# Another written order for the first 28 steps of a windowed-attention and feed-forward kernel

## The chip, the cores and the metric

The kernel runs on one core of a Trainium2 chip. The metric is the device time of one launch in microseconds (us); three runs of the kernel before the change took 841.5, 842.04 and 842.22 us. The core has five engines with their own instruction queues: PE (matrix products and the loads of their weights, which the profile lists as PEld), DVE (vector operations), ACT (activations and scaled copies), POOL, and SP, which in this kernel only issues transfers between the off-chip memory and the core. Each engine takes its instructions strictly in the order of its own queue and waits at an instruction until the semaphores that it names have been raised.

## The reference

Attention over 8 batches of 8 heads (576 positions, head width 64) with two kinds of window, and a feed-forward block with a gate on what comes out of it:

```python
scores = scale * np.matmul(q, k.transpose(0, 1, 3, 2))
mask_plain = (rel >= 0) & (rel < window)
mask_dil = (rel >= 0) & (rel < window * dilation) & (rel % dilation == 0)
...
attn = np.exp(scores - max) / sum
x = np.matmul(attn, v)            # 4608 tokens x 512
...
h = x @ w_in                      # 512 x 2048
g = h * np.clip(h + 3.0, 0.0, 6.0) / 6.0
return g @ w_out                  # 2048 x 512
```

## The kernel before

The attention is cut into 48 pieces called trios (192 positions of one kind of window for four heads each). The feed-forward block works on 12 chunks of 384 tokens, and its 2048 hidden columns are cut into 16 slices of 128. A step is one slice for one chunk: a first product (`gemm1`, 12 matrix products of 384 columns, L536 to L538), a gate on ACT and DVE (L544, L547, L551, L555), and a second product (`gemm2`, 9 products of 512 columns, L586 to L588). All large products are made from a high and a low half of each operand, three products for one.

A chunk can enter its first step only when the trios with its tokens have gone through attention and the slice of the weights has been loaded and converted. So the start of the kernel is a tangle of three chains, and its order is written out by hand: the string `ORDER` (L58 to L82), 588 names, is walked from left to right (L1275), and each name issues the instructions of one operation. ACT, DVE, SP and PE take their instructions in exactly the order in which they are issued there. What comes behind the first 28 steps is put in order by a planner (`_in_time`) and is not touched.

The names of `ORDER`, with t for a trio, m for a step and p for a half slice of the weights:

- On PE: `B`t makes the scores of trio t (L219, on top of a mask product at L328) and, from t = 2 on, between them the weighted values of an earlier trio (L229; `FOLLOW` at L57 names it). With one of the two it is 98 instructions, weight loads counted, with both 194, of 32 or 64 rows each. `V`t makes values alone (96). `E`t and `Y`t are three transposes each (L345, 6 instructions): of the exponents, and of the attention's output. `G`m is the first product of step m (24 instructions), `H`m the second (18).
- On DVE and ACT, for a trio: `R`, `S`, `X` (maximum, difference, exponent: L256, L260, L283), `CA` (copy of the transposed exponents, L358), `Z` (division by the sum, L304 to L307), `CX` (copy of the transposed output, L362), `XH`, `XL` (its high and low half, L438 and L444).
- On DVE and ACT, for half a slice of weights: `U`, `Q` (L490, L494, on ACT), `s`, `j`, `a` (L498, L504, L511, on DVE), `h` (L514, ACT) and `l` (L520, DVE). `RE`, `T`, `GH`, `GL` are the gate of a step.
- On SP: `k`t and `v`t load a trio's queries with keys and its values (416 and 390 KB; the tiles `first`, from t = 9 on `kq` and `v`), `w`p loads half a slice of weights (512 KB, tile `st`), `M0`, `M1`, `M2` three pieces of the masks (160, 24 and 432 KB). A name like `w0@R1` makes the transfer wait for `R1`. The transposes need `M1`, from which POOL makes the identity matrix (L762).

In the order before, the first four steps on PE are G0, G1, G2, G3, with B9 between G1 and G2 and B10 and B11 around G3; the first second product is H0.

Of the kernel before, what the change touches and what calls it, by code (L numbers as in the profile page):

```python
# [55 lines left out]

FOLLOW = {2: 0, 3: 1, 4: 2, 5: 3, 7: 5, 8: 6, 9: 7, 10: 8, 11: 9}  # L57
ORDER = """  # L58
k0 M0 M1 k2 k1 v0 k3 v2 B0 v1 k5 R0 S0 X0 E0 B1 CA0 B2 R1 S1 w0@R1 X1 Z0 E1 k4@X1 R2 CA1 Y0 v4@CA1 B3 S2 CX0 XH0
k6@S2 X2 XL0 v6@XL0 v3@XL0 Q0 U0 E2 s0 Z1 CA2 B4 R3 j0 S3 w2@j0 a0 X3 v5@a0 h0 Y1 Z2 B6 CX1 XH1 R4 Y2 R6 E3 CX2 XL1  # L60
CA3 S6 XH2 B5 S4 X6 w4@XH2 XL2 X4 Q2 l0 E6 U2 Z3 E4 k7@E6 CA6 R5 CA4 Y3 v7@CA6 s2 V4 CX3 S5 k8@CX3 XH3 j2 X5 XL3
v8@j2 Q4 E5 Z4 U4 w13@E5 CA5 a2 Y4 B7 s4 CX4 w6@a2 j4 h2 XH4 l2 k9@j4 B8 Z5 k10@l2 R7 Y5 XL4 w7@R7 CX5 Z6 G0 Q13 XH5
S7 w1@Q13 Q6 R8 X7 XL5 Y6 U6 S8 E7 G1 CX6 a4 CA7 s6 XH6 j6 X8 h4 XL6 B9 w5@G1 RE0 a6 RE1 l4 h6 k11@RE1 T0 E8 Q7 Z7
G2 CA8 GH0 R9 Q1 v9@GH0 GL0 U1 S9 U7 Y7 T1 B10 X9 s1 CX7 l6 GH1 v10@CX7 j1 XH7 E9 G3 R10 RE2 CA9 XL7 Q5 S10 U5 Z8
B11 X10 RE3 a1 GL1 h1 E10 T2 Y8 CA10 Z9 CX8 V10 GH2 R11 XH8 Y9 l1 CX9 Z10 H0 XH9 XL8 XL9 w3@XL8 S11 Y10 G8 GL2 CX10
w16@S11 T3 X11 s5 XH10 s7 GH3 XL10 E11 RE8 GL3 G6 CA11 j5 U3 w28@CA11 T8 Q3 a5 GH8 G10 j7 RE6 w11@GH8 h5 GL8 U16 T6
l5 Q16 G4 s16 GH6 a7 RE10 Q28 j16 v11@a7 h7 T10 H2 w8@j16 Q11 a16 U28 l7 h16 s3 H3 s28 GH10 GL6 l16 RE4 j3 Q8
w30@RE4 V11 U8 T4 GL10 GH4 G20 w17@U8 Z11 GL4 w9@Z11 a3 Y11 s8 RE20 G13 j28 CX11 h3 T20 XH11 j8 Q30 H4 XL11 U30 l3
w29@Q30 GH20 a8 Q17 a28 U17 H1 GL20 RE13 s17 h8 T13 Q9 j17 GH13 H8 U9 l8 w31@GH20 h28 GL13 Q31 a17 U31 G12 s9 l28
h17 Q29 j9 U29 l17 w14@GL20 G25 Q14 a9 RE12 s31 h9 s30 T12 U14 H20 l9 RE25 s14 GH12 T25 GL12 G5 w15@T25 j14 GH25 j31  # L70
GL25 a14 H13 RE5 a31 h14 T5 Q15 l14 U15 H12 j30 GH5 h31 s15 GL5 j15 G18 l31 w23@j14 Q23 a15 a30 h15 G11 s29 RE18 l15
h30 T18 l30 w18@U15 GH18 H10 j29 RE11 GL18 T11 a29 Q18 G27 GH11 U18 GL11 h29 s18 H18 l29 w19@T18 Q19 RE27 j18 U19
T27 a18 GH27 H25 s19 h18 GL27 l18 w10@Q18 Q10 U10 j19 H11 U11 s10 a19 s11 h19 j10 G22 l19 w12@a19 j11 a10 G15 RE22
a11 h10 T22 h11 l10 GH22 H6 l11 w20@j10 Q12 RE15 GL22 Q20 T15 U20 G14 GH15 s20 U12 GL15 j20 U13 s12 H22 RE14 a20 T14
h20 s13 GH14 l20 w21@l11 G7 Q21 GL14 U21 j13 j12 G24 a13 RE7 a12 h13 T7 h12 l13 w22@l20 H14 GH7 RE24 l12 GL7 T24 G17
s21 Q22 j21 GH24 U22 GL24 a21 U23 G16 RE17 s22 s23 h21 T17 j22 GH17 G9 l21 w24@l12 Q24 a22 U24 j23 h22 H24 s24 l22
j24 w25@l22 a23 H15 RE16 GL17 h23 a24 RE9 T16 h24 l23 G26 GH16 T9 Q25 GL16 U25 l24 w27@GH16 GH9 s25 G19 j25 a25 H17
h25 Q27 l25 H16 RE26 GL9 w26@H17 k12 k13 v12 v13 M2 RE19 T26 T19 G21 GH26 GH19 Q26 H9 U26 s26 U27 j26 H7
RE21 GL26 a26 T21 h26 GL19 H5 GH21 l26 GL21 s27 j27 G23 a27 h27 H21 l27 RE23 T23 GH23 H19 GL23 H23
"""  # L80


# [1456 lines left out]
```

## Time and profile before

| what | value |
|---|---|
| median of 3 runs | 842.04 us |
| the profiled execution | 846.16 us, of which the span of the trace is 844.0 us |
| mean granted PE clock | 0.990 |
| busy share of the span: PE, DVE, ACT, POOL | 98%, 77%, 68%, 7% |
| share of the chain that ended last that is PE's | 96% |
| PE instructions: products, weight loads | 8758, 8758 |
| read from and written to off-chip memory | 174.47 MB, 38.80 MB |

The span runs from the first to the last instruction in the trace; 2.2 us of the profiled execution lie around it. The rows of a view by stretches give for each engine its busy time and, in brackets, how many instructions fell into the stretch, then the granted PE clock, the busy share of the transfer engines and their rate.

### The profile page before, as it was taken

What the parts mean: (1) busy time and instruction counts of PE and PEld (TensorE: products, weight loads), DVE (VectorE), ACT (ScalarE), POOL (GpSimd) and SP (SyncE); (2) the same over time, 40 slices, a digit from 0 to 9 for tenths busy, and PEclk for the clock granted to TensorE, in tenths of its full rate; (3) what the DMA queues carried; (4) which work ended last, traced back from release to release, by engine and by line L of the source; (5) the groups of instructions that cost most, each with busy time, mean ns of one, the idle gap of its engine ahead of it and who ended that gap; (6) DMA issues with size and microseconds to landing.
All of it is one profiled execution on the core that took longest, in us unless ns stands there. A gap on an engine that the chain in (4) does not pass through costs nothing.

```text
span 844.0 us, 22143 instructions
## 1 busy us (share of the span) xinstructions
PE 828.2 (98%) x8758; PEld 776.8 (92%) x8758; DVE 646.7 (77%) x1313; ACT 573.7 (68%) x1400; POOL 55.5 (7%) x114
## 2 busy tenths in 40 slices
PE   7799999999999999999999999999999999999998
PEld 4589999898888889899899999999999999999997
DVE  4799988556677898888898777888677798445983
ACT  3688776334799885789985598855698755445552
POOL 0000000010222211000400001000001000000000
PEclk8799999999999999999999999999999999999999
DMA  8848332343778899899986898977789766996381
GB/s 280 275 134 251 124 122 84 115 152 115 229 233 267 290 345 378 280 391 392 389 295 233 285 347 298 340 249 258 272 313 319 255 228 234 336 368 219 131 293 57
DMA packets 115767, 214.70 MB, mean 254 GB/s; under 512 B 7504, under 2 KB 40272, under 8 KB 115664
## 3 DMA queue, kind: packets, MB, share of 16 engines
q1 hardware_dynamic: 115664, 213.29, 73.1%
q8 instruction: 69, 1.13, 0.5%
q14 instruction: 34, 0.28, 0.1%
HBM read 174.47 MB, written 38.80 MB: 253 GB/s over the span
## 4 chain that ended last, share of the span: by engine, by line
PE 96%; ACT 2%; issue 1%; DVE 1%; DMA 0%; SPq 0%; DVEq 0%
PE ps_o L736 28%; PE ps_x L745 9%; PE ps_x L747 9%; PE ps_x L746 9%; PE ps_h L536 6%; PE ps_h L537 5%; PE ps_h L538 5%; PE ps_o L586 5%; PE ps_o L588 5%; PE ps_o L587 5%; PE ps_b L237 2%; PE ps_a L219 1%; PE ps_a L229 1%; PE ps_b L219 1%; PE ps_a L237 1%; PE ps_a L345 1%
## 5 line engine op out<-in xcount | busy, mean ns | idle before, releaser
L736 PE MATMUL ps_o<-gh,ring 128*128 128x384 f32 x896 | 230.9, 334 | 0.5 <-ACT gh L1195 0.5
L736 PEld LDWEIGHTS ps_o<-gh,ring 128*128 128x128 f32 x896 | 161.9, 188 | 0.8 <-ACT gh L1195 0.8
L736 PE MATMUL ps_o<-gl,ring 128*128 128x384 f32 x448 | 149.9, 335 | 0.3 <-DVE gl L1199 0.2
L1199 DVE TENSOR_TENSOR gl<-g,gh 128x384 fp32r<-128x384 f32 x224 | 116.5, 553 | 28.2 <-ACT gh L1195 26.0
L1195 ACT CAST gh<-g 128x384 fp32r<-128x384 f32 x224 | 104.3, 513 | 27.8 <-PE ps_o L736 20.3
L745 PE MATMUL ps_x<-x,ring 128*128 128x384 f32 x256 | 88.5, 346 | 0.0
L536 PE MATMUL ps_h<-x,wi 128*128 128x384 f32 x256 | 88.3, 345 | 0.0
L537 PE MATMUL ps_h<-x,wi 128*128 128x384 f32 x256 | 86.4, 338 | 0.0
L538 PE MATMUL ps_h<-x,wi 128*128 128x384 f32 x256 | 86.4, 337 | 0.0
L746 PE MATMUL ps_x<-x,ring 128*128 128x384 f32 x256 | 86.2, 337 | 0.0
L747 PE MATMUL ps_x<-x,ring 128*128 128x384 f32 x256 | 86.1, 336 | 0.0
L736 PEld LDWEIGHTS ps_o<-gl,ring 128*128 128x128 f32 x448 | 84.1, 188 | 0.9 <-DVE gl L1199 0.9
L586 PE MATMUL ps_o<-wo,gh 128*128 128x512 f32 x192 | 75.1, 391 | 0.0
L587 PE MATMUL ps_o<-wo,gh 128*128 128x512 f32 x192 | 74.7, 389 | 0.0
L588 PE MATMUL ps_o<-wo,gl 128*128 128x512 f32 x192 | 74.7, 389 | 0.0
L544 ACT ACTIVATE t<-ps_h,three 128x384 f32<-128x384 f32 x64 | 37.0, 582 | 49.8 <-PE ps_h L538 49.0
L747 PE MATMUL ps_x<-cell,ring 128*128 128x384 f32 x192 | 64.8, 338 | 0.0
L746 PE MATMUL ps_x<-cell,ring 128*128 128x384 f32 x192 | 64.7, 337 | 0.0
L745 PE MATMUL ps_x<-cell,ring 128*128 128x384 f32 x192 | 64.7, 337 | 0.0
L1164 DVE TENSOR_TENSOR g<-g 128x768 f32<-128x768 f32 x64 | 60.8, 952 | 0.0
L547 DVE SCALAR_TENSOR_TENSOR t<-t,ps_h 128x384 f32<-128x384 f32 x64 | 35.0, 548 | 29.1 <-ACT t L544 28.7
L1049 DVE TENSOR_TENSOR s<-ps_x,s 128x384 f32<-128x384 f32 x64 | 35.2, 550 | 24.5 <-ACT s L1042 20.4
(114 smaller groups left out, 1765.4 us busy)
## 6 DMA issues: line engine op xcount, KB each, us to landing
ring<-sums SPq DMA_DIRECT2D x112, 512.0 KB, 8.0
ring<-rights SPq DMA_DIRECT2D x112, 512.0 KB, 6.7
st<-in_w SPq DMA_DIRECT2D x32, 512.0 KB, 4.1
kq<-in_qk SPq DMA_DIRECT2D x39, 416.0 KB, 4.8
v<-in_v SPq DMA_DIRECT2D x39, 390.0 KB, 5.8
sums<-wi SPq DMA_DIRECT2D x24, 256.0 KB, 7.1
rights<-wo SPq DMA_DIRECT2D x24, 256.0 KB, 5.4
out<-o SPq DMA_DIRECT2D x16, 384.0 KB, 2.9
```

The source lines that it names most:

```text
L536: nc.tensor.matmul(ph, lhsT=wt(f, 0)[:, ks], rhs=a, start=(kt == 0), stop=False)
L537: nc.tensor.matmul(ph, lhsT=wt(f, 0)[:, ks], rhs=b, start=False, stop=False)
L538: ins = nc.tensor.matmul(ph, lhsT=wt(f, 1)[:, ks], rhs=a, start=False, stop=(kt == NK - 1))
L586: nc.tensor.matmul(po[c][tt], lhsT=gh[:, rows], rhs=wt(f, 2), start=first, stop=False)
L587: nc.tensor.matmul(po[c][tt], lhsT=gh[:, rows], rhs=wt(f, 3), start=False, stop=False)
L588: return nc.tensor.matmul(po[c][tt], lhsT=gl[:, rows], rhs=wt(f, 2), start=False, stop=(f == NF - 1))
L736: nc.tensor.matmul(banks[part][:, :CH], lhsT=right[:, a, cols], rhs=x, start=(start and not i), stop=(i == 2), skip_group_check=True)
L745: nc.tensor.matmul(bank, lhsT=tile_[:, 0, ks], rhs=h[:, kt], start=(start and kt == 0), stop=False, skip_group_check=True)
L746: nc.tensor.matmul(bank, lhsT=tile_[:, 0, ks], rhs=l[:, kt], start=False, stop=False, skip_group_check=True)
L747: nc.tensor.matmul(bank, lhsT=tile_[:, 1, ks], rhs=h[:, kt], start=False, stop=(kt == 1), skip_group_check=True)
L1195: nc.scalar.copy(two[0], gated_tile(g, q, k))
L1199: nc.vector.tensor_tensor(out=two[1], in0=gated_tile(g, q, k), in1=two[0].bitcast(F32), op=ALU.subtract)
```

## The change

Only the string `ORDER` is another. It holds the same 588 names, so every instruction and every transfer is there as before; what changes is where each stands in its engine's queue, and which of the transfers wait for which operation. The first line of the old table and of the new one:

```diff
-k0 M0 M1 k2 k1 v0 k3 v2 B0 v1 k5 R0 S0 X0 E0 B1 CA0 B2 R1 S1 w0@R1 X1 Z0 E1 k4@X1 R2 CA1 Y0 v4@CA1 B3 S2 CX0 XH0
+k0 M0 k1 B0 R0 w6 k2 M1 U6 v3 S0 X0 v0@R0 B1 w2@B1 R1 E0 S1 X1 s6 E1 CA0 v1 U2 k3 B2 j6 CA1 s2 R2 w0 B3 S2 Z0 Q6 k6 Q2
...
```

On SP, the first transfers before were the following rows; here `in_qk` is a `k`, `in_v` a `v`, `in_w` a `w` and `in_mask` a piece of the masks:

```order
L190 DMA first<-in_qk 128x832
L759 DMA mi<-in_mask 32x2560
L759 DMA mi<-in_mask 96x128
L190 DMA first<-in_qk 128x832 x2
L199 DMA first<-in_v 128x780
L190 DMA first<-in_qk 128x832
L199 DMA first<-in_v 128x780 x2
L190 DMA first<-in_qk 128x832
L475 DMA st<-in_w 128x1024
```

And after the change:

```order
L190 DMA first<-in_qk 128x832
L759 DMA mi<-in_mask 32x2560
L190 DMA first<-in_qk 128x832
L475 DMA st<-in_w 128x1024
L190 DMA first<-in_qk 128x832
L759 DMA mi<-in_mask 96x128
L199 DMA first<-in_v 128x780 x2
L475 DMA st<-in_w 128x1024
L199 DMA first<-in_v 128x780
L190 DMA first<-in_qk 128x832
L475 DMA st<-in_w 128x1024
```

The first load of weights (now `w6`) moved from the eleventh transfer to the fourth, two more (`w2`, `w0`) stand among the first twelve, `M1` moved from the third to the sixth, and `k3`, which was the seventh, is now the eleventh.

On PE, the first product G0 stood before behind block B8, the last one that reads a tile `first`, and the transposes Y5 (`x` is the output of attention, `ps_h` the bank of the first product):

```order
L229 MATMUL ps_a<-first,a 32x65
L219 MATMUL ps_a<-first 32x64
L345 MATMUL ps_a<-ident,x 128x128 x3
L536 MATMUL ps_h<-x_78,wi 128x384
L537 MATMUL ps_h<-x_84,wi 128x384
L538 MATMUL ps_h<-x_78,wi 128x384
```

After the change the first product is G1, and this stands ahead of it:

```order
L229 MATMUL ps_a<-first,a 32x65
L219 MATMUL ps_a<-kq 32x64
L345 MATMUL ps_a<-ident,e 128x128 x3
L536 MATMUL ps_h<-x_78,wi 128x384
L537 MATMUL ps_h<-x_84,wi 128x384
L538 MATMUL ps_h<-x_78,wi 128x384
```

One more block, B9, which reads `kq`, and the transposes E7, Y6 and E8 have moved ahead of the first product. In PE's queue the blocks and transposes follow each other now as B0 B1 E0 E1 B2 B3 Y0 B6 E3 E2 B5 Y1 B4 Y3 E5 Y2 B7 E6 E4 V4 B8 E7 Y4 Y5 Y6 B9 E8, then G1 Y7 B10 E9 G0 Y8 B11 G2 Y9 E10 G3 V10 E11 and then G6. Before they were B0 E0 B1 B2 E1 Y0 B3 E2 B4 Y1 B6 Y2 E3 B5 E6 E4 Y3 V4 E5 Y4 B7 B8 Y5, then G0 Y6 E7 G1 B9 E8 G2 Y7 B10 E9 G3 B11 E10 Y8 V10 Y9 and then H0.

At the head of ACT's queue the first exponent stood alone; now a conversion of weights (L490, `U6`) stands ahead of it, and `U2`, `Q6`, `Q2` and `U0` stand among the operations of trios 0 to 3.

More of the change, by code (lines that the diff above doesn't have):

```diff
@@ L58 @@
 ORDER = """
-k0 M0 M1 k2 k1 v0 k3 v2 B0 v1 k5 R0 S0 X0 E0 B1 CA0 B2 R1 S1 w0@R1 X1 Z0 E1 k4@X1 R2 CA1 Y0 v4@CA1 B3 S2 CX0 XH0
[L60 to L78, printed above, removed]
@@ L79 @@
-RE21 GL26 a26 T21 h26 GL19 H5 GH21 l26 GL21 s27 j27 G23 a27 h27 H21 l27 RE23 T23 GH23 H19 GL23 H23
+k0 M0 k1 B0 R0 w6 k2 M1 U6 v3 S0 X0 v0@R0 B1 w2@B1 R1 E0 S1 X1 s6 E1 CA0 v1 U2 k3 B2 j6 CA1 s2 R2 w0 B3 S2 Z0 Q6 k6 Q2
+j2 U0 w16@U2 s0 w4 R3 Y0 CX0 k5@S0 S3 j0 Q0 B6 X3 X2 v2@X2 Z1 U4 E3 a2 k4 s4 R6 E2 CA3 j4 U16 B5 S6 Q4 v6 v5@CA0 CA2
+Y1 h2 a4 B4 Z3 Y3 R5 CX1 XH1 l2 h4 S5 X6 X5 l4 E5 Z2 XH0 R4 k7@Z3 XL1 a0 CX3 S4 CA5 XH3 Y2 CX2 B7 v4 v8@X2 E6 XL3 XH2
+X4 k8@j4 w28@XH3 CA6 R7 v7@XH0 E4 XL0 S7 XL2 CA4 V4 a6 Z5 B8 Q28 Z4 h0 Z6 R8 X7 s16 E7 w1@s4 k9@a6 Y4 U28 S8 w3 Y5 l0
@@ new lines @@
+CA7 CX4 Y6 B9 XH4 w30@Z5 XL4 R9 X8 Z7 U30 U3 CX5 S9 k10@XH4 E8 G1 Y7 k11 M2 CA8 B10 X9 XH5 s28 s30 h6 j16 CX7 s3 XL5
+l6 Z8 XH7 RE1 j3 E9 G0 Q3 Y8 Q16 v9@S8 CA9 w5@B10 CX6 j30 XL7 R10 T1 v10 S10 CX8 B11 XH6 Z9 v11@XH7 G2 Q30 R11 XL6 X10
+Y9 w8@B11 RE0 E10 T0 S11 XH8 G3 RE2 CX9 XH9 CA10 X11 Q1 V10 T2 RE3 XL8 E11 XL9 a16 j28 Q5 w14@Q30 w18 h16 G6 GH1 Q14
+G4 RE6 U1 T3 a28 Z10 G8 T6 w17@CA10 a3 l16 a30 h28 U5 GH0 CA11 l28 V11 RE4 h3 w7@E9 s1 T4 U14 j1 RE8 Z11 h30 G13 T8 U8
+RE13 Q8 a1 Y11 w10@Q8 Y10 s14 G25 CX11 GL0 h1 GH4 G10 U17 Q7 s8 T13 RE25 l3 l1 H0 U7 j14 w31@h1 s17 j8 CX10 a14 w29
@@ new lines @@
+l30 T25 G20 a8 GL1 RE10 h8 T10 h14 l8 Q17 Q18 l14 RE20 s7 s5 GL4 T20 GH3 w9 XH10 U9 H1 j7 j17 a7 GL3 h7 G5 s9 Q9 w15
+l7 U29 j5 a17 H4 a5 U18 G12 s18 RE5 GH2 j18 H3 G11 G27 h17 U31 RE12 Q29 h5 j9 U10 s29 T5 a18 T12 GH8 l5 w19@H3 GH12
+GL8 s10 h18 U15 GH20 GL2 a9 s31 XL10 RE27 U19 j31 l18 j29 RE11 h9 T27 GH25 Q19 H2 s15 j15 H8 l17 w20@U10 T11 a29 GL20
+h29 GL25 G18 Q15 l29 j10 RE18 s19 w22@Q29 j19 Q10 G22 a10 T18 a15 l9 U20 h10 h15 w11@s29 GL12 GH13 a19 H20 Q31 RE22
+G15 w12@G18 l15 H25 GH11 T22 l10 s20 U22 GL11 a31 RE15 w13 U11 h31 s22 h19 G14 s11 T15 j20 Q20 a20 l19 j11 H12
@@ new lines @@
+w21@GL11 GH6 l31 Q11 h20 G7 a11 RE14 GL6 H11 j22 w25 Q12 Q22 T14 RE7 U12 GH22 l20 T7 s12 Q21 j12 GL22 GL13 H6 a12 a22
+U13 w24@Q20 Q13 GH10 s13 GH18 h12 GL18 G17 h11 l11 G24 RE17 h22 U21 l12 H18 H13 RE24 j13 s21 G9 T17 j21 T24 GL10 Q25
+U25 l22 a13 s25 H10 h13 RE9 GH24 v12@RE9 l13 a21 h21 U24 T9 G26 G16 GL24 j25 l21 Q24 GH14 RE26 w23@h20 a25 s24 j24
+GH27 Q23 U23 a24 RE16 s23 h25 w26@l13 T26 GL14 j23 a23 H24 T16 l25 h24 GH15 H22 G19 GH16 GL16 GH9 GL9 h23 w27@Q24 U26
+l24 H14 Q26 G21 RE19 GL15 RE21 H16 l23 U27 s26 Q27 j26 a26 h26 T19 s27 l26 GH19 H9 GH17 H15 GH5 T21 G23 j27 GH21 GL21
@@ L80 @@
+GL19 a27 GL5 XH11 RE23 T23 GH7 H19 GL7 h27 GH23 H21 GH26 k13@H9 v13@G21 XL11 GL17 l27 GL27 H5 H7 k12@GH19 GL23 GL26
+H23 H17
 """
```

## The prediction

> **What bounds the kernel now.** I read the page first, then the view of waits, for the time behind 58 us and for the first 60 us.
>
> ```profile
> PE 828.2 (98%) x8758; PEld 776.8 (92%) x8758; DVE 646.7 (77%) x1313; ACT 573.7 (68%) x1400; POOL 55.5 (7%) x114
> ```
>
> PE is the bound. Behind 58 us it waits twice, for 0.7 us in all:
>
> ```profile
> PE ps_o L736 <- ACT gh L1195: 0.5, 1, 0.5
> PE ps_o L736 <- DVE gl L1199: 0.2, 1, 0.2
> ```
>
> All that an order of the first steps can win or lose lies ahead of that. There the same view says (engine, line, what was waited for, us, times, longest):
>
> ```profile
> PE ps_a L219 <- issue: 3.8, 3, 1.5
> PE ps_a L345 <- ACT e L283: 1.9, 1, 1.9
> PE ps_a L229 <- issue: 1.4, 1, 1.4
> PE idle L162 <- DVE zeros L159: 1.3, 1, 1.3
> PE ps_a L345 <- DVE x L307: 1.3, 3, 0.7
> PE ps_a L229 <- ACT a L358: 1.3, 3, 0.7
> ```
>
> The largest item, 5.2 us, is "issue": PE waits for nothing that is in the program. The chain of work shows where:
>
> ```profile
> 18.57 1.49 issue
> ...
> 24.41 0.94 issue
> ...
> 28.93 1.39 issue
> ...
> 36.15 1.36 issue
> ```
>
> I cut the time at the ends of these four waits (20.06, 25.35, 30.31, 37.51) and let the view by stretches count instructions:
>
> ```profile
> 1.30:15.23 13.93, 11.57 (x219) 6.79 (x222) 4.16 (x9) 2.93 (x6) 0.29 (x1) 0.75 0.86 310
> 15.23:20.06 4.83, 2.68 (x136) 2.05 (x136) 2.93 (x8) 2.69 (x6) 0.00 (x0) 1.00 0.93 285
> 20.06:25.35 5.29, 3.99 (x127) 2.88 (x127) 5.09 (x13) 4.30 (x12) 0.00 (x0) 1.00 0.77 257
> 25.35:30.31 4.96, 3.31 (x127) 2.65 (x127) 4.25 (x12) 4.05 (x11) 0.00 (x0) 1.00 0.75 220
> 30.31:37.51 7.20, 5.16 (x126) 3.44 (x126) 5.44 (x15) 3.18 (x8) 0.00 (x0) 0.60 0.97 337
> 37.51:45.98 8.47, 8.46 (x126) 8.01 (x127) 5.79 (x13) 5.36 (x12) 0.00 (x0) 0.73 0.60 201
> ```
>
> From one wait to the next there are 127 products and 127 weight loads, then 127 and 127, then 126 and 126: nearly the same number each time, though the program does something else in each. The page has a queue that fits:
>
> ```profile
> q8 instruction: 69, 1.13, 0.5%
> ```
>
> 1.13 MB in 69 packets is 16.4 KB each. I conclude that PE's instructions come in blocks of about 256, and that from 15.23 to 37.51 the next block came too late four times. **The attention part is paced by the supply of instructions**: 4.83, 5.29, 4.96 and 7.20 us for a block. The first three average 5.03. The slow one is the stretch in which transfers held their engines for 0.97 of the time.
>
> [...]
>
> **The change, part by part.** No instruction is added or removed. From the order of PE I count instructions. Before, the block edges seen above are numbers 449 (in B3), 705, 961, 1217 and 1473 (in B8), and H0 begins with number 2470. After, number 449 is again in B3, 31 behind its start, and 1729 is in B9, 1985 in B10, 2241 in B11; G6 begins with 2476. Ahead of G6 stand the same operations as ahead of H0 before, plus E11 (6 instructions). So I compare the start of G6 with the start of H0 plus one E, from these rows:
>
> ```profile
> 50.23 0.33 PE ps_a L345 x3
> ...
> 57.38 0.94 PE ps_a L229 x46
> 58.32 0.48 PE ps_a L345 x3
> 58.80 0.41 PE ps_o L586
> ```
>
> 58.80 and 0.33: **59.1 us** is what the new order has to beat. Behind it PE's work is the same, and it hardly waits.
>
> *To number 449.* B3 needs `k3`, now the eleventh transfer. Up to it go four `k`, three `v`, two `w`, M0 and M1: 4 x 416 + 3 x 390 + 2 x 512 + 184 = 4,042 KB or 4.14 MB. At the 310 GB/s of the first stretch from 1.30 on they are there at 14.7, and 31 instructions later it is 15.0; before it was 15.23. This hides the other edits at the start. U6 ahead of the first exponent X0 waits for the fourth transfer, 1.54 MB, at about 6.3. M1, now sixth, is there after 1.99 MB at 7.7, and `v0`, the eighth, after 2.79 MB at 10.3. Each may hold up E0 or B2 by about a microsecond, but B3 cannot start ahead of 14.7 anyway; without that cover they would cost that microsecond. The conversions that come earlier fall where DVE and ACT are busy for 4.16 and 2.93 of 13.93 us, so I cost them at nothing.
>
> *The waits that transfers now have.* SP's queue stands still at each of them, so I ask whether the loads behind it still come in time.
>
> ```profile
> L511 DVE CUSTOM_DVE_ANT_0 va<-va 128x1024 uint16<-128x1024 uint16 x32 | 21.4, 683 | 0.1
> ...
> L256 DVE TENSOR_REDUCE mx<-ps_a 128x6 f32<-128x384 f32 x12 | 6.6, 550 | 8.5 <-PE ps_a L219 8.3
> L260 DVE TENSOR_TENSOR e<-ps_a,mx 128x384 f32<-128x384 f32 x12 | 6.5, 552 | 0.1
> L283 ACT ACTIVATE e<-e 128x384 f32<-128x384 f32 x12 | 6.2, 522 | 10.4 <-DVE e L260 10.4
> ...
> L444 DVE TENSOR_TENSOR x<-xf,x 128x96 fp32r<-128x96 f32 x12 | 3.5, 330 | 0.0
> ```
>
> ```profile
> kq<-in_qk SPq DMA_DIRECT2D x39, 416.0 KB, 4.8
> ...
> first<-in_v SPq DMA_DIRECT2D x9, 390.0 KB, 5.2
> ```
>
> The tightest is `v2@X2`, with `k4`, `v6` and `v5` behind it. X2 stands behind X3 on ACT, and X3 waits for B3, whose other 163 instructions end at 16.4 to 17.1. R3, S3, X3 and X2 (0.55, 0.55, 0.52, 0.52) make it 18.5 to 19.2, `v2` lands 5.2 later, `k4` about one more: 24.7 to 25.4. B4 waits for both, and its instruction 961 is due at 25.1 by the sum below: between nothing and 0.7 late. `k9@a6` holds B9 in the same way. B7 ends about a microsecond behind number 1217, on DVE R7, S7 and XL0 at 0.55, XL2 in three pieces at 0.33 and a6 (L511) at 0.68 take 3.4, the load 4.8: 9.2 behind 1217, where 1729 is due 10.1 behind it. I give them no term of their own; the one slow block of the sum below is where such a wait goes, and a second one is a rival.
>
> *From 449 to 2241.* Seven refills. Before, four followed each other at this pace, because G0 comes behind only 1,648 instructions; now G1 comes behind 1,860, and G1 and G0 are alone between blocks. Does the work fit under the refill? A pair block and a product of 384 columns at full clock are:
>
> ```profile
> 54.67:56.27 1.60, 1.60 (x99) 1.33 (x98) 1.60 (x4) 1.38 (x3) 0.00 (x0) 1.00 0.08 22
> ```
>
> ```profile
> 48.13 0.18 PE ps_h L536
> 48.30 0.17 PE ps_h L537
> ```
>
> From 1729 to 1985: 125 of 194 instructions of B9 (1.03), E8 (0.33), G1 (12 x 0.175 = 2.10), Y7 (0.33), 95 of B10 (0.78): 4.57 us. From 1985 to 2241 it is 4.58 in the same way. Both are under the fastest refill, 4.83, so these two are still paced by the refill and no faster than that. I take 4.83 for them, since the rate of transfers fell to 0.60 by then before. The other five lie in the time of heavy loading. The bounds for one are 4.83 and 7.20; before, one of four was slow. I take four at 5.03 and one at 7.20. The sum: 15.0 + 20.1 + 7.2 + 9.7 = 52.0.
>
> *From 2241 to G6.* 73 of 194 of B11 (0.60), G2 and G3 (4.20), Y9, E10, E11 (0.99), V10 (0.94): 6.7 us.
>
> **The sum** is 58.7, against 59.1: **0.4 us less**. What before lost at low clock and in waits behind 37.51 is won, and the three more blocks at the refill's pace give it back. The profiled execution took 846.16 us (span 844.0) and would take 845.8; on the median of 842.04 I carry over the difference: **841.6 us**. I call 0.2% (1.7 us) about what a measurement can tell.
>
> **The rivals.**
>
> *No slow block* (chance 0.29). The slow one before fell into a stretch in which PE also waited for data; if it was that, the five take 5.03 each, and the sum is 56.5, 2.6 less: 839.4. With all seven at 4.83 it would be 55.5: 838.4, the lower end. Against it: the transfers are as many and are packed no less.
>
> *Low clock at the first products* (0.15, the slower side). Before, PE ran at low clock in a stretch around G0:
>
> ```profile
> 30.00:40.00 10.00, 7.64 (x222) 5.76 (x223) 6.34 (x18) 3.49 (x9) 0.00 (x0) 0.59 0.98 346
> ```
>
> ```profile
> 32.06 0.87 PE ps_a L345 x3
> 32.93 0.43 PE ps_a L328
> ...
> 35.37 0.43 PE ps_a L328
> ...
> 41.34 0.32 PE ps_h L536
> ```
>
> Then a product takes 0.32 instead of 0.175, a pair block 2.44 (from 32.93 to 35.37), three transposes 0.87. While blocks wait for their instructions that costs nothing. But from 1729 on, at 42.3 in my sum, the work up to 1985 would be 1.57 + 0.87 + 3.84 + 0.87 + 1.19 = 8.3 us instead of 4.83: 3.5 more, 845.1 us. The point from which it decides: low clock still on behind 42.3. Before, it ended at about 42. For it speaks that the thin stretches, PE busy about half of the time, go on longer now.
>
> [...]
>
> *A second slow block* (0.10): 7.20 instead of 5.03, 2.2 more, 843.8, just slower. It decides from two of seven on.
>
> *Refills hidden* (0.03). Then the transfers would bound: twelve `k`, nine `v`, nine `w`, M0 and M1 up to `k11`, 13,294 KB or 13.6 MB, at 310 GB/s 45.2 us; with B11 (1.60) and the 6.1 us behind it that is 53: about 836. The four waits of before speak against it.
>
> **How the numbers follow.** The forecast has 0.43 and stays within 0.2%. Faster are the first and the last rival: 0.32. Slower are the low clock and the second slow block: 0.25. The range of 838.8 to 845.1 takes in each case's own time but the last, and leaves out the fastest part of the first.
>
> **What would show it.** In the profile after: waits called issue on PE, each about 254 instructions behind the one before, some six in B6, B4, B7, B8, B9 and B10; number 449 at about 15; the first L536 at 43 to 44; G6 (the fifth group of twelve products) at 58.7; no wait of PE behind it that was not there before. It would be wrong if the stretches between the waits were not of equal count, if B9 or B10 waited for a transfer for over a microsecond, or if DVE came late for a second product behind 59 us.

## The result, and the profile after

The kernel after took 850.48 us (median of 6 runs, 849.12 to 851.95), the kernel before beside it 842.13 us (6 runs, 840.75 to 843.72). The ratio is 1.0097, with a 95% interval of 1.008 to 1.0115: **1% slower**, where the forecast was 841.6 us and the range ended at 845.1.

The page of the profile after, first row:

```profile
PE 828.8 (98%) x8758; PEld 777.3 (92%) x8758; DVE 646.8 (76%) x1313; ACT 572.7 (68%) x1400; POOL 56.1 (7%) x114
```

PE is still the bound and as busy as before. The view of waits of PE, over the whole span (engine, line, what was waited for, us, times, longest):

```profile
PE ps_a L219 <- issue: 6.3, 3, 2.8
PE ps_a L345 <- POOL ident L762: 2.6, 1, 2.6
PE idle L162 <- DVE zeros L159: 1.3, 1, 1.3
PE ps_a L219 <- DMA first<-in_qk: 1.1, 2, 0.9
PE ps_a L229 <- DMA first<-in_v: 1.1, 1, 1.1
PE ps_a L229 <- ACT a L358: 0.6, 1, 0.6
PE ps_o L736 <- ACT gh L1195: 0.5, 1, 0.5
```

The waits for instructions are there (6.3 us), and a new one of 2.6 us: E0 waits for the identity matrix, which POOL makes from M1. Behind the first 63 us PE waits as little as before. I cut the time at the block edges, that is where PE goes from one block of 256 instructions into the next (numbers 449, 705, 961 and so on to 2497; in the first profile of before the four waits for instructions end at 705, 961, 1217 and 1473, each 256 behind the one before). These numbers count all instructions in PE's queue, also the 27 ahead of H0 that are neither products nor weight loads and mostly wait for a semaphore. The prediction left these out, so that H0, its number 2470, is number 2497 here. The view by stretches says:

```profile
1.30:16.20 14.90, 10.00 (x219) 5.59 (x225) 4.73 (x9) 4.80 (x9) 0.64 (x1) 0.86 0.93 325
16.20:22.70 6.50, 3.73 (x137) 2.91 (x138) 5.47 (x14) 3.27 (x7) 0.00 (x0) 0.76 0.81 295
22.70:28.65 5.95, 5.95 (x127) 4.28 (x126) 3.77 (x9) 3.14 (x7) 0.00 (x0) 0.50 0.67 250
28.65:34.04 5.39, 3.50 (x132) 2.59 (x128) 5.30 (x13) 5.19 (x15) 0.00 (x0) 0.96 0.88 303
34.04:40.00 5.96, 3.36 (x128) 2.60 (x127) 4.65 (x13) 3.01 (x6) 0.00 (x0) 0.94 0.82 282
40.00:45.76 5.76, 5.76 (x127) 4.75 (x128) 3.64 (x10) 2.17 (x6) 0.00 (x0) 0.50 0.60 228
45.76:50.44 4.68, 4.68 (x132) 4.21 (x127) 3.37 (x10) 3.42 (x8) 0.00 (x0) 0.96 0.72 226
50.44:55.78 5.34, 5.04 (x145) 4.36 (x130) 5.27 (x14) 4.91 (x13) 0.00 (x0) 1.00 0.93 275
55.78:62.63 6.85, 6.85 (x128) 6.38 (x127) 6.09 (x17) 5.50 (x16) 0.00 (x0) 1.00 0.69 218
```

The blocks are of equal count, as forecast, but of the seven up to 55.78 all but one take longer than the 5.03 of the sum (the other, from 45.76 on, took 4.68), and two of them run wholly at half clock (0.50). G6 begins at 62.77 us, where the sum had 58.7.

These two profiles show less than half of the loss. The execution of after took 849.41 us and that of before 846.16: 3.3 us apart, where the medians are 8.35 apart. The executions of before spread from 840.03 to 846.27 us in one series of 29; the one profiled lies at the upper end of that. Two further profiles of before took 842.73 and 842.62 us, and a second one of after 852.05. The number to compare is that of instruction 2497, since from there on all five need 786.8 to 787.6 us to their end:

| profile | time, us | number 1473 | number 2497 |
|---|---|---|---|
| before, first | 846.16 | 37.51 | 58.71 |
| before, second | 842.73 | 34.91 | 55.59 |
| before, third | 842.62 | 35.11 | 54.98 |
| after, first | 849.41 | 40.00 | 62.63 |
| after, second | 852.05 | 40.76 | 64.70 |

So against the second and third profile of before the loss is 7 to 10 us, made ahead of 2497, of which five to six lie ahead of 1473 and two to four behind it.

### The profile page after: what moved, and what is told of

It is laid out like the page before. It is cut to its first block, busy times and chain, and to the rows that moved or that the text cites. A ratio compares the mean times of both kernels' runs of the same rounds, so it can differ in the third digit from the quotient of the medians.

```text
span 847.6 us, 22130 instructions
## 1 busy us (share of the span) xinstructions
PE 828.8 (98%) x8758; PEld 777.3 (92%) x8758; DVE 646.8 (76%) x1313; ACT 572.7 (68%) x1400; POOL 56.1 (7%) x114
## 4 chain that ended last, share of the span: by engine, by line
PE 94%; DMA 2%; ACT 1%; issue 1%; DVE 1%; SPq 0%; DVEq 0%
PE ps_o L736 28%; PE ps_x L745 9%; PE ps_x L747 9%; PE ps_x L746 9%; PE ps_h L536 5%; PE ps_o L586 5%; PE ps_o L588 5%; PE ps_o L587 5%; PE ps_h L538 5%; PE ps_h L537 5%; PE ps_b L237 2%; DMA first<-in_qk 1%; PE ps_b L219 1%; PE ps_a L237 1%; PE ps_a L219 1%; PE ps_a L229 1%
```

## The experiments

All are other strings in the place of `ORDER`, with the same 588 names and so the same instructions. Ratios are to the kernel before, run on the same chip in the same series (its medians there: 842.4 to 843.4 us).

### The two kernels again

No edit.

> The kernel before, unchanged, for a second profile. The profiled execution of before took 846.16 us, but its 29 timed ones 840.03 to 846.27. If the first 60 us differ from run to run, in how long refills wait and where the low clock falls, the number 2497 (58.71 us in the first profile) comes as much earlier as the time is shorter: 55 to 56 us at 842 to 843, and all behind it takes 787 us as before.

> The kernel before once more, unchanged, for a third profile: the same as for the second one, number 2497 at the time of the run less 787.4 us.

> The kernel after, unchanged, for a second profile. If its waits for instructions (6.3 us in the first one) belong to the order, they come again: at least 4 us of issue waits ahead of 60 us, and number 2497 at the time of the run less 786.9 us. If they were chance, as four of them were in the first profile of before (5.2 us, against none and 1.1 us in the second and third), they fall below 2 us.

The waits of PE in the second profile of before:

```profile
PE ps_a L345 <- ACT e L283: 4.2, 3, 1.9
PE ps_a L345 <- DVE x L307: 2.0, 3, 0.8
PE idle L162 <- DVE zeros L159: 1.3, 1, 1.3
```

and the first and the fourth row of the same view of the second profile of after:

```profile
PE ps_a L219 <- issue: 4.2, 4, 1.7
...
PE ps_a L229 <- issue: 1.9, 1, 1.9
```

Before has no wait for instructions at all here, and 1.1 us in its third profile, against 5.2 in the first. After has 6.3 and 6.1. What I took for the pace of the kernel before was the luck of one execution; of the kernel after, both profiles have it.

### Fewer and more transfers in flight, in the kernel before

The names of transfers in SP's order, `b_thin`, `b_flood` and `b_group` against before:

```diff
...
-w13@E5 w6@a2 k9@j4 k10@l2
+w13@h2 w6@XH4 k9 k10
...
```

```diff
...
-w0@R1 k4@X1 v4@CA1 k6@S2 v6@XL0 v3@XL0 w2@j0 v5@a0 w4@XH2
+w0 k4 v4 k6 v6 v3 w2 v5 w4
...
```

```diff
-w0@R1 k4@X1 v4@CA1 k6@S2 v6@XL0 v3@XL0 w2@j0 v5@a0 w4@XH2 k7@E6 v7@CA6 k8@CX3 v8@j2 w13@E5 w6@a2 k9@j4 k10@l2
+w0@R1 k4 v4 k6 v6@XL0 v3 w2 v5 w4@XH2 k7 v7 k8 v8@CX3 w13 w6 k9 k10
...
```

> The kernel before, with four of its transfers issued later: w13 behind h2, w6 behind XH4, then k9 and k10, so that none of them is issued between instruction 1217 (30.31 us in the trace of before) and 33 us. Theory 'queue': a block of PE's instructions is asked for when PE enters the block ahead of it, and its packet waits behind the transfers that have been issued by then or soon after. Then the slow refill of before (7.20 us, its packet 4.84 us behind the edge, with eight transfers in flight) falls to about 5.0: number 1473 at about 35.4 instead of 37.5, H0 at 56.5 to 57 instead of 58.7, and 1.5 to 2 us less, 840.3 us at 842.1 for before. Rival 'fixed': a refill takes what it takes, whatever is in flight, and what made the after kernel slower is its later start and its three more blocks; then 1473 stays at 37.5 and the time at 842.1.

844.23 us, ratio 1.0016 (0.9996 to 1.0037): not faster. No wait for instructions is left and 1473 comes at 34.09, but there were none in the second profile of before either, and what is left took over:

```profile
PE ps_a L345 <- ACT e L283: 5.2, 3, 2.4
PE ps_a L345 <- DVE x L307: 2.1, 3, 0.9
```

> The kernel before, with the waits taken off nine transfers (w0, k4, v4, k6, v6, v3, w2, v5, w4), so that SP issues the first nineteen one after the other, by about 10 us. They hold 7.54 MB, at 310 GB/s until about 25.6 us. Theory 'queue': the packet that holds number 449 is asked for at about 9.9 and comes behind all of them: 449 at 26 to 27 us instead of 15.2, the blocks behind it then every 4.0 to 4.5 us since little is in flight, G0 at about 47 instead of 40, and some 5 to 7 us more, 847 to 849. Rival 'shared': the packet takes turns with the transfers, and a deeper queue costs it little: 449 by 16 us, the blocks as before, 842 us or, as data come no later, slightly less.

844.44 us, ratio 1.0025 (1.0005 to 1.0045). Neither theory as stated: number 449 came at 15.49, not at 26, so the packet doesn't stand behind all that was issued; but 705 came 6.39 us behind it, with one wait of 3.5 us:

```profile
PE ps_a L219 <- issue: 3.5, 1, 3.5
```

> The kernel before with the way in which after issues its transfers: one wait for three to five of them (w0, k4, v4, k6 behind R1; v6, v3, w2, v5 behind XL0; w4, k7, v7, k8 behind XH2; v8, w13, w6, k9, k10 behind CX3), each earlier than before or as it was, and none later. Order and operations as they were. Theory 'queue': five or more transfers are in flight when 705, 1217 or 1473 is asked for; their packets start 3 to 4 us behind the edge, issue waits of 3 us or more come in an execution whose like had none and 1.1 us, and the time is 1.5 to 3.5 us longer, 845 to 846.5. Rival 'data': transfers that are issued earlier cost nothing; 842.5 to 843.5.

844.34 us, ratio 1.0014 (0.9993 to 1.0036), inconclusive. The waits of 3 us that "queue" expected did not come: its profile, with one of 1.1 us, lies among those of before. It is that of its fastest execution, though (842.49 us; the slowest took 849.46). So grouping alone is not shown to cost anything in the order of before.

### The start, and the early weights

`a_start` moves M1 to the third place and v3 behind k3 (first diff); `b_w` puts w6 and w16 early into before (second); `a_w` loads and converts w6 and w16 late in after (third, transfers only), and `a_w_start` joins it with `a_start`.

```diff
-k0 M0 k1 w6 k2 M1 v3 v0@R0 w2@B1 v1 k3 w0 k6
+k0 M0 M1 k1 w6 k2 v0@R0 w2@B1 v1 k3 v3 w0 k6
...
```

```diff
-k0 M0 M1 k2 k1 v0 k3 v2 v1 k5 w0@R1 k4@X1 v4@CA1
+k0 M0 M1 w6 k2 k1 v0 k3 v2 v1 k5 w0@R1 k4@X1 w16 v4@CA1
...
```

```diff
-k0 M0 k1 w6 k2
+k0 M0 k1 k2
...
-k6 w16@U2 w4 k5@S0
+k6 w4@U2 k5@S0
...
-v7@XH0 w1@s4 k9@a6 w3 w30@Z5 k10@XH4
+v7@XH0 w6@s4 w1 k9@Z5 w3 w30@Z5 w16 k10@XH4
...
```

> The kernel after, with M1 third instead of sixth, k1 and k2 behind it, and v3 behind k3 instead of ahead of v0: E0 no longer waits for the identity matrix, and B3 gets k3 1.2 us earlier. Both theories have number 449 at about 15.0 instead of 16.20. Theory 'queue': the transfers in flight at that moment end when they did, so the packet for 705 starts at about 20 as it did (20.31), 705 comes at 22.3 or later instead of 22.70, and of the 1.2 us at most 0.4 is left: 850.1 us at 850.5 for after. Rival 'fixed': all blocks come 1.2 earlier, G6 at 61.6 instead of 62.77, 849.3 us.

849.13 us, ratio 1.0071 (1.005 to 1.0093). Number 449 came at 15.25, and 705 at 21.05 instead of 22.70: the gain of the start was not eaten at the next block. That part of the theory "queue" fell. Two edits are joined here; `k3` landed at 15.13 instead of 16.08, and 449 followed that landing by 0.1 us in both.

> The kernel before with two weight loads early, as after has them: w6 fourth in SP's queue and w16 behind k4; nothing else moves (their conversions stay where they were). Theory 'bytes': up to about 30 us PE is fed at the rate of the transfers, so 512 KB that no pair block needs cost 1.7 us at 310 GB/s, and both 3.4: number 705 two to three us later than in the second and third profile of before (19.1 us), 2 to 3.4 us slower, 844.5 to 846. Rival 'order': what costs in after is the order of the blocks and conversions on PE, DVE and ACT; then this stays at 842 to 843.

845.04 us, ratio 1.002 (1.0006 to 1.0034): 1.6 us more in the medians, where "bytes" expected 2 to 3.4. Number 705 came at 21.59, about 2.5 later, as it expected.

> The kernel after with w6 and w16 loaded late (w6 ahead of w1, w16 behind w30), their conversions moved with them behind 38 us; the order of all else as in after. Theory 'bytes': k3, M1 and all behind them land 1.7 us earlier, and from w16's old place on 3.4 us: 449 at about 14.7, 705 at about 19.7 to 20.5 (22.70 in after), 1217 at 31, number 2497 at 59.5 to 60, 847 to 848 us. Rival 'order': 705 and what follows come as in after, 850 us.

849.34 us, ratio 1.0067 (1.0041 to 1.0094). 449 came at 16.07 and 705 at 22.38, against 16.20 and 22.70: hardly a gain there. "Bytes" missed: with w6 gone from its place, `k3` still landed at 15.95.

> As the one before, with M1 third, k1 and k2 behind it, and v3 behind k3. Theory 'bytes': about one more us at the start, 846 to 847 us; what is left against before (842 to 843) is the late part, B9 to B11 with fewer large products between them, which cost 2.3 us from number 1473 to 2497 (22.6 us in after, 20.3 in the second profile of before). Rival 'order': 849, as with the early M1 and k3 alone.

849.26 us, ratio 1.0058 (1.0038 to 1.0078). That is clear of the interval of after, but not of the one of `a_start`. So the early weights cost 1.6 us in the order of before, but in the order of after they are not shown to be more than a small part of the loss.

### The waits of the transfers in the kernel after

`a_thin` puts the transfers in groups behind the block edges; `a_spread` gives nearly each a wait of its own:

```diff
-w0 k6 w16@U2 w4 k5@S0 v2@X2 k4 v6 v5@CA0 k7@Z3 v4 v8@X2 k8@j4 w28@XH3 v7@XH0 w1@s4 k9@a6 w3 w30@Z5 k10@XH4 k11 M2 v9@S8
+w0 k6 w4@S2 w16@j2 k5@R3 v2@j0 k4@X2 v6@R6 v5@S6 k7@CA2 v4@CX1 k8@l4 w28@CA5 v7@XH3 w1@XL3 v8@R7 k9@a6 w30@X7 w3@Z6 k10@XH4 k11@CA8 M2 v9@X9
```

> The kernel after, with the transfers from w0 to v9 issued a few at a time behind the block edges instead of early: w16 and w4 behind j2, v5, k7 and v4 behind CA3, v6, k8 and w28 behind CA5, v7, k9, w3 and w1 behind CA6, w30, k10 and v8 behind CA7, k11, M2 and v9 behind CA8. Operations on PE, DVE and ACT stand as in after. Theory 'queue': with one or two transfers in flight when a block is asked for, instead of three to five, its packet starts 1 to 2.5 us behind the edge instead of 2.8 to 4.1, and a block takes 4.3 to 5.0 us instead of 5.3 to 6.5: seven blocks win 4 to 6 us, G6 at 57 to 59 instead of 62.8, and 845 to 847 us. Rival 'fixed': the blocks take as long as they did, and data come later: 850.5 us or more.

849.39 us, ratio 1.0075 (1.005 to 1.0101). The waits for instructions fell to 1.8 us, but waits for `a`, `in_qk` and `e` grew to 3.3, 2.2 and 1.8: what was saved on instructions was lost on data.

> The kernel after with the same operations on PE, DVE and ACT and the early weights and the late M1 as they are, but with a wait of its own on nearly every transfer from w4 to v9 (w4 behind S2, w16 behind j2, k5 behind R3, v2 behind j0, k4 behind X2, v6 behind R6, v5 behind S6, k7 behind CA2 and so on) in place of one wait for three or four of them: each is issued about when the one ahead has landed, not later than needed. Theory 'queue': one to three transfers in flight at a block edge instead of three to five; the refills start 1 to 2 us behind the edge instead of 3 to 4, issue waits fall from 6.2 us to below 2.5, number 1473 comes at 36.5 to 38 instead of 40.0 and 40.8, and the time falls to 847 or 848. Rival 'order': the chain through DVE, ACT and the data of this order is as long; the issue waits fall, waits for data and for ACT grow by as much, 849 to 850.5 us.

848.6 us, ratio 1.0056 (1.0037 to 1.0074): clear of after's interval, 3.5 us better by the ratios and 1.9 by the medians. Its waits:

```profile
PE ps_a L345 <- POOL ident L762: 2.5, 1, 2.5
PE ps_a L219 <- issue: 2.2, 2, 1.4
PE ps_a L219 <- DMA first<-in_qk: 2.0, 4, 1.1
...
PE ps_a L229 <- issue: 1.1, 2, 0.7
```

3.3 us for instructions instead of 6.3, and number 1473 at 36.68 instead of 40.00. In this profile spreading wins most of the early loss, and the edit touches nothing but when and in which order transfers are issued. From 1473 to 2497 it takes 24.86 us, though, where after took 22.63.

> The kernel after with w6 and w16 late, M1 third and v3 behind k5 (each alone or together these left it at 849.1 to 849.3), and with the transfers spread as in the run named a_spread. Theory 'queue': its two slow refills (3.98 and 3.91 us behind the edge, with seven and six transfers in flight) become 1.5 to 2.5, the waits for in_qk (3.3 us) are the ones left; 844.5 to 846.5 us. Rival 'order': 848.5 or more.

849.56 us, ratio 1.0066 (1.0043 to 1.0089): missed. With v3 behind k5 and the late w6 PE waits 2.4 us for `in_v` and 1.5 for `kq`.

### Early part and late part

`h_ab` has after's order ahead of B7 and before's behind it; `b_late` is before with G0, G1 and w5 behind B9:

```diff
...
-G0 Q13
+Q13
...
-E7 G1 CX6
+E7 CX6
...
-B9 w5@G1
+B9 G0 G1 w5@G1
...
```

> A hybrid: the order of after as far as it stands ahead of B7 (about 32 us of its trace, seven of the twelve pair blocks), and all that is left in the order of before, with G0 and G1 between B8 and B9 again. Theory 'early': the loss is made in the first 32 us (M1 and k3 late, weights loaded early, more low clock); then the hybrid is as slow as after, 849 us. Theory 'late': the loss is made behind 32 us, where B9, B10 and B11 come with fewer products of 2.1 us between them and so wait for their instructions; then it is within 1.5 us of before, 841 to 844.

> The kernel before with G0 and G1 (and the transfer w5, which waits for G1) moved behind B9 on PE, so that ten pair blocks stand ahead of the first large product as in after; nothing else moves. Theory 'late': B9 now waits for its instructions (number 1729 cannot come before 42 us) and for E7, and the 4.2 us of G0 and G1 no longer lie beside a refill: 3 to 4 us slower than before, 845.5 to 846.5. Theory 'early': what stands ahead of 32 us is unchanged, so is the time, 842 to 843.

850.01 us, ratio 1.0081 (1.0063 to 1.01), and 848.45 us, ratio 1.0064 (1.0043 to 1.0084). Each alone costs most of what the whole change does; I had expected one of them to. The stretches ahead of and behind 1473, first of the second profile of before, then of after, `h_ab` and `b_late`:

```profile
1.30:34.91 33.61, 28.33 (x728) 19.10 (x728) 20.00 (x50) 17.23 (x39) 0.29 (x1) 0.75 0.84 281
34.91:55.59 20.68, 19.10 (x508) 16.90 (x508) 19.18 (x46) 16.92 (x39) 0.00 (x0) 1.00 0.64 223
```

```profile
1.30:40.00 38.70, 26.54 (x730) 17.96 (x730) 23.92 (x56) 19.41 (x42) 0.64 (x1) 0.81 0.84 299
40.00:62.63 22.63, 22.33 (x508) 19.69 (x508) 18.37 (x48) 16.00 (x40) 0.00 (x0) 0.86 0.73 235
```

```profile
1.30:40.65 39.35, 27.64 (x728) 18.57 (x728) 22.41 (x53) 19.30 (x43) 0.62 (x1) 0.77 0.80 276
40.65:60.67 20.02, 19.78 (x512) 17.74 (x511) 17.08 (x44) 15.42 (x36) 0.00 (x0) 0.94 0.62 185
```

```profile
1.30:36.40 35.10, 26.65 (x728) 17.98 (x728) 21.79 (x54) 16.95 (x39) 0.29 (x1) 0.83 0.89 302
36.40:62.52 26.12, 23.57 (x507) 20.06 (x507) 17.03 (x40) 17.27 (x40) 0.00 (x0) 0.78 0.37 132
```

The counts of instructions are the same. `h_ab` loses all of its time ahead of 1473 and is as quick as before behind it; `b_late` loses nearly all behind 1473, at a granted clock of 0.78 instead of 1.00: its first two large products begin at 45.3, in a stretch of half clock that lasted until 48.0.

> The hybrid h_ab (after's order ahead of B7, before's order behind it; 850.0 us) with its transfers from w4 to w7 issued one at a time, as in a_spread. If the early loss is that of transfers in flight at the block edges, and the late one that of large products coming late, this hybrid has neither: number 1473 at 36.5 to 37.5 (40.65 in h_ab, 36.68 in a_spread), 20.3 us from there to 2497 as in before, and 844 to 845.5 us. If spreading only moves the wait, 848 or more.

848.0 us, ratio 1.0061 (1.0042 to 1.0081). Number 1473 came at 40.86: spreading did not help this hybrid early on (it waits 3.7 us for `in_qk`, 2.8 for the identity), so it could not show what it was made for.

### One more large product beside the pair blocks

A pair block is a `B` that makes scores and values, 194 instructions. `a_dense` is `a_spread` with G2 ahead of B11, `a_all` has the start of `a_start` as well:

```diff
...
-h6 j16 CX7 s3 XL5 l6 Z8 XH7 RE1 j3 E9 G0 Q3 Y8 Q16
+h6 RE1 j16 CX7 s3 XL5 l6 T1 Z8 XH7 j3 E9 G0 Q3 Y8 G2 Q16
...
-R10 T1 v10
+R10 T0 v10
...
-v11@XH7 G2 Q30
+v11@XH7 Q30
...
-RE0 E10 T0 S11
+E10 S11
...
```

and RE0 now stands behind CA9.

> The kernel a_spread (848.6 us) with G2 ahead of B11 on PE, and for it RE1 and T1 behind G1 and RE0 and T0 behind G0, so that the buffers of its products are free. In a_spread B11 waits for its instructions and the packet of block 2241 comes 4.08 us behind the edge. Theory 'cover': the loss of the late part is that only two large products stand beside the last pair blocks, where before has four; G2 in that gap wins up to its 2.1 us: 846.5 to 847.5. Rival: the end is set by something else behind it (gates on ACT and DVE, V10, E11); 848.6.

> The kernel a_dense with M1 third and v3 behind k3 as in a_start (which alone won 1.35 us). If the three causes add up (start 1.35, spread 1.9, cover up to 2): 845 to 846 us at 850.5 for after and 843.2 for before. If they are one and the same wait seen at three places, 847.5 or more.

846.97 us, ratio 1.0047 (1.003 to 1.0064), and 848.02 us, ratio 1.0061 (1.0043 to 1.0078). The first met its number, and is better than after by 3.5 us in the medians; against `a_spread` alone the intervals overlap. Its profile (848.57 us, 1.6 above its median) does not show the gain where it was expected: from 1473 to 2497 it takes 24.80 us, as `a_spread` does with 24.86. So the number was met, but not shown to be met for the reason given. The second shows that the parts don't add up. No version was faster than before.

## Why the prediction was wrong

*That PE is the bound, that PE's instructions come in blocks of 256, and that all is decided in the first steps*: right. PE is busy for 98% of the span in both; the four waits of the first profile of before end 256 instructions apart, and queue q8 moved 69 packets of 16,384 bytes; every profile ends 787 to 788 us behind number 2497.

*The number to beat, 59.1 us*: **wrong, and some two fifths of the error.** It was read in an execution that took 4.1 us longer than the median. I named that gap and carried the difference over, as if it lay elsewhere; it lay in the very stretch that I compared. In the two other profiles number 2497 is 3.1 and 3.7 us earlier, and so the time to beat was 55.4 to 56.0. The sentence "the attention part is paced by the supply of instructions" held for that one execution. In the others PE waits for the chain of exponents (4.2 and 2.9 us for `e`, 2.0 and 2.1 for `x`), which I took for small.

*To 449, 15.0 us*: came at 16.20 and 17.00. The cover that I named (k3) landed at 16.08 instead of 14.7; w0 and k6, issued 0.5 and 1 us behind it, were in flight beside it, which the sum left out. PE waited 2.6 us for what is made from M1, costed at nothing, but the cover held: behind that wait PE waited 1.1 us more for `v0`, and the chain that ended last up to 16.2 goes through `k1`, the wait of w2 and `k3`, not through M1. In `a_start` the two edits gave back 0.95 at number 449 and 1.35 us in the median, though the intervals of the two ratios overlap.

*The refills, four at 5.03, one at 7.20, two at 4.83*: **wrong in size.** Counted from one block edge to the next, the seven took 39.6 us in the first profile (16.20 to 55.78) and 40.9 in the second (17.00 to 57.88), against 37.0 in the sum. The miss lies in the five under heavy loading, 29.6 and 30.4 us where the sum had 27.3; the two from 1729 to 2241, 10.0 and 10.5 us, came near their 9.7. And 4.83, which I took for the fastest refill, is no floor: in the second profile of before the block from 961 on took 3.8 us. What I had not read is when the packets of the refills start. The records of queue q8 in 20 profiles of this study, seven refills in each (numbers 705 to 2241), give the time from the entry into a block to the start of the packet with the next one, by the number of transfers that were issued (SP was done with the instruction) and not landed at the entry:

| transfers in flight | refills | packet behind the edge, us: median (range) | next block entered within 1.65 us of the packet's end |
|---|---|---|---|
| 0 | 8 | -0.8 (-2.2 to 0.7) | 0 |
| 1 | 11 | 1.1 (-1.2 to 2.2) | 2 |
| 2 | 33 | 1.3 (-0.4 to 4.3) | 8 |
| 3 | 42 | 2.4 (0.9 to 6.9) | 24 |
| 4 | 26 | 3.1 (1.3 to 4.8) | 18 |
| 5 and more | 20 | 3.7 (2.6 to 4.4) | 16 |

In the first profile of after the packets of the five refills from 705 to 1729 took 0.93 to 0.97 us each, and PE entered the blocks 1.2 to 1.45 us behind their ends. With four in flight a block took 5.7 us (median), with more 6.3, and PE had to wait for the next one in 34 of 46; with none or one it was there in time in 17 of 19.

The entry is a mark to count from, not shown to be the moment at which the block is asked for: in 16 of the 140 the packet started ahead of it. And the number in flight is not the whole account. In each row the packets of the kernels that begin with the order of after start later than those with the order of before, by 0.5 us or more (medians of 3.1 and 2.0 us at three, 3.4 and 2.4 at four); why stays open.

The order after sets one wait ahead of three or four transfers, and they are issued 0.5 to 2 us ahead of an edge: in its first profile five, four, two, five and three are in flight at the entries into the blocks that begin with 449, 705, 961, 1217 and 1473. `a_spread` shows that the way in which the transfers are issued is a cause: it changes nothing else, and 1473 comes 3.3 us earlier. The four kernels with that spreading (`a_spread`, `a_dense`, `a_all`, `a_w_spread`) take 20.8 to 22.1 us from 449 to 1473 in their profiles; the two profiles of after and the three kernels that keep its grouping (`a_start`, `a_w`, `a_w_start`) take 22.8 to 24.2. That it works through the number in flight is shown only in part: at the five entries `a_spread` has two, three, four, four and four, which is clearly fewer at the first alone, and its packets start 1.8, 4.5, 2.2, 3.2 and 3.1 us behind them instead of 4.1, 3.6, 3.0, 3.8 and 3.6. `b_flood` shows another limit: with eight in flight at 15.49 the packet started at 19.31, while they landed until 23.5; it does not wait for all of them.

From 63 us on no wait for instructions is left in the first profile of after (PE waits there for 0.7 us in all, for `gh` and `gl`): the blocks of large products last for 14.1 us (62.63 to 76.76) and more.

*From 1729 to 2241, and the rival "low clock at the first products"*: its point of decision, half clock behind 42.3, came true: it lasted until 46.2 in the first profile of after and came again from 47.3 to 50.7 in the second. Its price, 3.5 us on the block from 1729 to 1985, did not. Number 1729 came later too, at 45.76 and 47.4. In the first profile that block took 4.68 us at a granted clock of 0.96; the half clock lay in the block before it, which ended 1.3 us behind its packet, so that the refill alone can account for its length. In the second it took 5.9 us instead of 4.83, with half clock for 3.4 of them. So about one of the 3.5 us is seen, in one profile of two. I gave the rival 0.15, though thin stretches, which I had named in its favour, were what my own forecast had most of.

The next table splits the time of each profile, by the records of PE: gaps in which neither a product nor a weight load runs, and half of the busy time at granted clock 0.5, since a product of 384 columns took 0.32 us there and 0.175 at 1.0 (the records of the clock begin at 4.5 to 7.1 us; that the time ahead of the first counts at 0.5 is an assumption, which no record shows); what is left is 18 to 20 us in each part, the work itself. Half clock beside a refill that is still on its way need not cost anything of its own, so the columns say where the time went, not what each would give back.

| profile | to 1473: gaps + half clock | 1473 to 2497: gaps + half clock |
|---|---|---|
| before, first | 9.3 + 7.0 | 0.2 + 2.3 |
| before, second and third | 5.0 + 10.0; 6.6 + 8.3 | 1.6 + 0.0; 0.3 + 0.5 |
| after, first and second | 11.9 + 8.0; 9.5 + 11.9 | 0.2 + 3.1; 1.9 + 3.3 |
| `h_ab` | 11.4 + 9.3 | 0.2 + 1.1 |
| `b_late` | 8.2 + 7.4 | 2.5 + 5.0 |
| `a_spread` | 8.0 + 8.3 | 2.2 + 3.4 |
| `a_dense` | 10.2 + 5.2 | 2.7 + 3.3 |

Early, after loses 20 to 21 us where before typically loses 15, and `a_spread` and `a_dense` 15 to 16. Late, it loses 3 to 5 where before loses 1 to 2.5. What brings the half clock is not shown: in the second profile of after the granted clock was 0.5 from 9.8 to 26.8 us, and PE's longest wait behind 3 us was 2.5.

*Why the first large product comes late*, which my sum had at 43 to 44, and not its price: in after it begins at 47.2 and 49.3 us, in the two later profiles of before at 36.5 and 37.0. It needs XL4, which ended at 45.8 and 46.6 instead of 36.8 and 37.1, some 20 us behind the landing of k4 in each: 25.1 and 26.2 instead of 16.6 and 16.4. PE does not wait for it at G1, since the end of B9 and E8 still stand ahead of G1 in its queue; that the late k4 is the cause is argued, not shown. Two large products stand ahead of B11 instead of four. That this placing costs much by itself in the order of before is shown by `b_late`; that it is what the late part of after loses is not shown, since with G2 ahead of B11 the late part still takes 24.8 us (`a_dense`) and with all three edits 24.5 (`a_all`). An order after with trio 4 as early as before, which would test it directly, was not tried.

*Refills hidden, a second slow block*: the first did not come; the second is what the refills did (in the first profile the five blocks up to 45.76 took 5.4 to 6.5 us), with the wrong picture of one slow block among good ones.

**In sum**: of the 8.35 us between the medians about 3.5 are the number to beat, 1.2 to 2.0 the start, and 2.6 to 3.9 the seven refills, with the half clock among them. Some 4 us of the loss were won back by no edit, and how they divide between the refills, the chain to XL4 and the clock stays open.

## What to carry to other kernels

Before a forecast rests on waits in the stretch that the change touches, compare the profiled execution with the median: a gap of 4 us that lies in that stretch is part of the answer, not an offset. Where short instructions run beside heavy loading, count the transfers in flight at each block edge, and try a wait of its own for each transfer rather than one wait for four of them: here that won 1.9 us in one order, with more time lost further on, and nothing clear of noise in two others. And where small work leaves PE thin, ask what the granted clock will be when the first large product begins (in `b_late` it was half, and 0.78 in the mean from 1473 to 2497), and how many of them stand beside the small work.

## What was not expected of the hardware

One program differs by 6 us from one execution to the next (840.03 to 846.27 us), all of it ahead of number 2497 as far as three profiles show. The granted clock fell to half in stretches of about 3.4 us or multiples of it (6.8, 10.2, 13.7, 17.1), at other places in each profile: 7.9 to 14.7 and 31.8 to 42.0 in the first of before, 8.0 to 25.1 in the second. And instructions did not always come ahead of data: with three transfers in flight a packet of 16,384 bytes started up to 6.9 us behind PE's entry into the block ahead of its own.
